# Fused attention, gated MLP and channel mix on one core: accumulator banks for turned blocks, a new layout of the first batch's work, and raw w_k loads behind gate weights

## The chip, the cores and the metric

The kernel runs on one core of a Trainium2 chip. The metric is the device time of one execution in microseconds, the median of several runs. Matmuls run on TensorE (PE in the profile, its weight loads PEld), the rest on VectorE (DVE), ScalarE (ACT) and GpSimd (POOL). SyncE (SP) issues every DMA of this kernel, in order.

## The reference

Three parts, all in fp32, with B = 4 batches, H = 8 heads, S = 576 positions, D = 64, model width 512, inner width 1024:

```python
# attention with a decay bias
cum = cumsum(max(s, 0)); bias = min(-(cum[q] - cum[k]), 0)
attn = softmax(where(causal, -1e9, q @ k.T / 8 + bias)); x = attn @ v      # -> [B, S, 512]
# gated MLP
h = gelu_tanh(x @ w_in); u, v = h[:, :512], h[:, 512:]
v_s = w_sg @ layernorm(v, g_ln) + b_sg          # mixes positions
x = x + (u * v_s) @ w_out
# channel mix
xk, xr = lerp(x, shift(x), mu_k), lerp(x, shift(x), mu_r)
out = sigmoid(xr @ w_r) * (max(xk @ w_k, 0) ** 2 @ w_v)
```

## The kernel before

**Precision.** A product of two fp32 operands is made of fp32r parts: a rounded high part and the rest (`split_lo`, L69: x minus high, 1 instruction). `gemm3` (L374) adds high·high, high·low and low·high in one PSUM bank. Weights come in as 64-bit words; `convert` (L75) makes them into high and low parts with three ScalarE instructions (L77, L82, L88) and three VectorE ones (L83, L85, L70).

**Attention** (`attn_pair`, L213). 16 pairs of heads, four per batch; the first batch has pairs 0 to 3. For each head the transposed k and q come in (`kq`), upper and lower halves are copied and shifted by DMA into `qa`, `ka`, `QB`, `KB`, low parts are split off (mostly on GpSimd), and the sums of `s` go into spare rows by two small DMAs. Scores of a block row of 128 queries go to a PSUM bank `sc`; VectorE adds the mask and takes the minimum (L284), ScalarE takes the exponential with its sum (L292). Each block row is then turned by TensorE against the identity (L307, L310, L318) into a bank `tp` (or `tq`) and copied to `pt1` or `pt2` (L312 to L321). `i` counts the block rows 0 to 4; the last is 64 rows of both heads together. The sums are turned too (`rt`, L324), inverted, written to DRAM and read back broadcast (`rb`), and multiply `x_t` at L361.

**Gated MLP** (`moe1`, L381), once for each batch: `xs` is the split x (L395, L396), `xq` its last 64 columns side by side (L398). Five `v` products, gelu, statistics (L424, L425), a power on GpSimd (L426, L427), the normalisation at L428, cast (L430) and split (L432). Then eight `u` products, eight spatial products `sg`, the gate (L468 to L471) and eight `o` products. The weights of u and o come in eight blocks `wc` of 512 KB through three buffers: the first batch converts them itself (`first_wc`, L179) and writes them to DRAM, the later ones load them from there (`load_wc`, L513). Blocks 0 to 3 serve u, 4 to 7 serve o. For the first three batches gelu is made of Square, Tanh and two VectorE steps (L501); the last batch uses the chip's own gelu.

**Banks.** PSUM has eight banks: three `sc`, two `tp`, three `acc`. `bank` (L367) gives `moe1` only `acc` in the first three batches and all eight in the last one. `tq`, `pv` and, in the first batch, fourth and fifth block tiles and `rt` are `acc` as well; in later batches those tiles and `rt` are `tp`.

**Order.** `attention_until` (L544) interleaves the generators: attention leads the MLP by `LEAD` heads (0.75), with costs `A_COST` and `E_COST`. The prologue (L151) runs beside the first batch's attention: step 0 to 3 convert the four parts of `w_in` for v, 4 to 6 the first three `wc`, 7 to 11 load and split the spatial weights (`spatial`, L198). `PRO` (L542) says at how many finished heads the first seven steps come; step 2 also writes the sums to DRAM and loads four constants (L160). A scheduler then places the instructions of all engines by a timeline of its own; `after` (L495) adds an order to it, no semaphore.

**Channel mix.** `late(i)` (L577) loads the raw w_k (i below 8) and w_r through two buffers `lraw` and converts them; conversions 4 to 7 are held behind the last normalised cast of the last batch. `mixed` makes x tiles, `dense` the products k and r; the rest is a product in seven parts with w_v.

```python
    PRO = [0, 0] + [0.5 + 0.75 * i for i in range(5)]
    ...
            attention_until((b + 1) * H + LEAD + RATE[b] * H * e_done / E_COST)
            if pro is not None and next(pro, None) is None:
                pro = None
    ...
        raw = lk.tile([P, 512, 2], U32, tag="lraw", name=f"lraw{i}", bufs=2)
        nc.sync.dma_start(out=raw.rearrange("p n c -> p (n c)"), in_=src.bitcast(U32))
```

Of the kernel before, what the change touches and what calls it, by code (L numbers as in the profile page):

```python
# [8 lines left out]
F32 = mybir.dt.float32  # L9
F32R = mybir.dt.float32r  # L10
U32 = mybir.dt.uint32
AF = mybir.ActivationFunctionType
ALU = mybir.AluOpType

B, H, S, D = 4, 8, 576, 64
DM, DFF = 512, 1024
FH = DFF // 2
P = 128
# [12 lines left out]
QS = 256  # L31
# [7 lines left out]
def fused_kernel(ctx, tc, kqT, vL, s, w_in, g_ln, w_sgT, b_sg, w_out, mu_k, mu_r, w_k, w_v, w_r, out):  # L39
    nc = tc.nc  # L40
# [5 lines left out]
    wscr = dram.tile([8, P, 2 * KD * P], F32R, tag="wscr", name="wscr")  # L46
# [18 lines left out]
    def f32(ap):  # L65
        return ap.bitcast(F32)


    def split_lo(eng, lo, x, hi):  # L69
        eng.tensor_tensor(out=lo, in0=x, in1=f32(hi), op=ALU.subtract)  # L70
# [25 lines left out]
    psum1 = banks1.enter_context(tc.tile_pool(name="psum1", bufs=3, space=bass.MemoryType.PSUM))  # L96
# [17 lines left out]
    wsg = [ew.tile([P, NT, S], F32R, tag=f"wsg{i}", name=f"wsg{i}") for i in range(2)]  # L114
# [83 lines left out]
    def spatial(k):  # L198
        raw = ep.tile([P, TW1], F32, tag="tmp", name=f"wsr{k}", bufs=3)[:, :S]
        if k < 4:  # L200
            nc.sync.dma_start(out=raw, in_=w_sgT[k * P:(k + 1) * P])
        else:
            nc.sync.dma_start(out=raw[0:64], in_=w_sgT[512:])
            nc.sync.dma_start(out=raw[64:128], in_=w_sgT[512:])
        nc.scalar.copy(wsg[0][:, k], raw)
        split_lo(nc.gpsimd, wsg[1][:, k], raw, wsg[0][:, k])

    xT = {}

# [3 lines left out]
    def attn_pair(b, hp):  # L213
# [3 lines left out]
        for hh in range(2):  # L217
            h = 2 * hp + hh
            hd = b * H + h

            kq = at.tile([P, S], F32, tag="kq", name=f"kq{hd}", bufs=2)
            nc.sync.dma_start(out=kq, in_=kqT[b, h])
            i = hd % (NSET + 1) if first else hd % NSET
            qb, kb = QB[i], KB[i]

            csrc = cr[hd:hd + 1] if b == 0 else cumd[hd]
            nc.sync.dma_start(out=f32(qb[1:4:2]), in_=f32(csrc))
            last_row[0] = nc.sync.dma_start(out=f32(kb[0:3:2]), in_=f32(csrc))
            if i < NSET:
                qa = at.tile([P, S], F32R, tag="qa", name=f"qa{hd}")  # L230
                ka = at.tile([P, S], F32R, tag="ka", name=f"ka{hd}")
            else:
                qa, ka = qaf, kaf
            (nc.scalar.copy if hd < 2 else nc.gpsimd.tensor_copy)(qb[64:128], kq[64:128])  # L234
            (nc.vector.tensor_copy if 1 < hd < 4 else nc.scalar.copy)(ka[0:64], kq[0:64])  # L235
            nc.sync.dma_start(out=f32(qa[0:64]), in_=f32(qb[64:128]))
            nc.sync.dma_start(out=f32(ka[64:128]), in_=f32(ka[0:64]))
            lo = nc.vector if hd in (0, 2) else nc.gpsimd
            split_lo(lo, qa[64:128], kq[64:128], qb[64:128])
            split_lo(lo, kb[64:128], kq[0:64], ka[0:64])  # L240
            ops.append((qa, ka, qb, kb))
            if hh == 0:
                vf = at.tile([P, 2, NT, D], F32, tag="vf", name=f"vf{pr}", bufs=2)
                nc.sync.dma_start(out=vf, in_=vL[b][:, h:h + 2])
                x_t = ep.tile([P, S], F32, tag="xT", name=f"xT{pr}", bufs=8)
                xT[(b, hp)] = x_t
            yield 0
# [14 lines left out]
        for hh, i in steps:  # L262
# [38 lines left out]
            if i == 0:  # L301
                st0 = st
                continue
            tag = "acc" if first and i > 2 else "tp"
            tp = psum1.tile([P, 512], F32, tag=tag, name=f"tp{pr}_{hh}_{i}", bufs=3 if tag == "acc" else 2)
            if i == 1:
                nc.tensor.transpose(tp[:, 0:P], st0[:, 0:P], ident)  # L307
# [3 lines left out]
            if i == 1:  # L311
                (nc.vector.tensor_copy if first and not hh else nc.scalar.copy)(pt1[:, hh], tp[:, :QS + P])  # L312
            elif i < 4:
                (nc.vector.tensor_copy if i == 2 and not first else nc.scalar.copy)(
                    pt2[:, hh, :i + 1, q0 - QS:w - QS], tp[:, :(i + 1) * P].rearrange("p (j m) -> p j m", m=P))
            else:
                tp4 = psum1.tile([P, 512], F32, tag="acc", name=f"tq{pr}", bufs=3)
                nc.tensor.transpose(tp4[:, 0:P], st[:, 512:640], ident)  # L318
                for a in range(2):
                    nc.scalar.copy(pt2[:, a, :4, q0 - QS:], tp.rearrange("p (j a m) -> p a j m", j=4, a=2)[:, a])  # L320
                nc.vector.tensor_copy(pt2[:, :, 3, 0:64], tp4[:, :P].rearrange("p (a m) -> p a m", a=2))  # L321
            yield (i + 1) * 200
        rt = psum1.tile([P, 512], F32, tag="acc" if first else "tp", name=f"rt{pr}", bufs=3 if first else 2)
        nc.tensor.transpose(rt[:9, :P], sm, ident)  # L324
        rc = at.tile([9, P], F32, tag="rc", name=f"rc{pr}")
        nc.vector.tensor_scalar_add(rc, rt[:9, :P], SUM_EPS)
# [54 lines left out]
    def moe1(b):  # L381
# [13 lines left out]
            nc.scalar.copy(xs[0][:, k], xT[(b, k)])  # L395
            split_lo(nc.vector if b == 0 else nc.gpsimd, xs[1][:, k], xT[(b, k)], xs[0][:, k])  # L396
        for i in range(2):
            nc.vector.tensor_copy(xq[:, :, i], f32(xs[i][:, :, 512:]))  # L398
        yield 0
        v = ep.tile([P, NT, FH], F32, tag="v", name=f"v{b}")  # L400
        st6 = ep.tile([P, NT, 6], F32, tag="st6", name=f"st6_{b}")
# [3 lines left out]
        for t in range(NT):  # L405
# [13 lines left out]
            else:  # L419
# [5 lines left out]
            nc.vector.bn_aggr(out=mv[:m, t], in_=st6[:m, t])  # L425
            nc.gpsimd.tensor_scalar_add(rstd[:m, t:t + 1], mv[:m, t, 1:2], LN_EPS * GS * GS)  # L426
            nc.gpsimd.tensor_tensor(out=rstd[:m, t:t + 1], in0=rstd[:m, t:t + 1], in1=mhalf[:m, 0:1], op=ALU.pow)  # L427
            nc.vector.tensor_scalar(out=v[:m, t], in0=v[:m, t], scalar1=mv[:m, t, 0:1], scalar2=rstd[:m, t:t + 1],  # L428
                                    op0=ALU.subtract, op1=ALU.mult)
            last_cast[0] = nc.scalar.copy(vn[0][:m, t], v[:m, t])  # L430
            if t < 4:
# [59 lines left out]
    exps = []  # L491
    last_gate = [None]
    last_cast = [None]

    def after(late, early):  # L495
        tc.add_manual_dep(late.ins, early.ins.name, mybir.DependencyInfo(mybir.DependencyClass.NoSync, mybir.DependencyReason.DATA),
                          reason="order")
# [15 lines left out]
    def load_wc(b, c):  # L513
        if b == 0:
            if c >= 3:
                first_wc(c)
            return wc0[c]
        wc = ew.tile([P, 2, KD * P], F32R, tag="wc", name=f"wc{b}_{c}", bufs=3)
        nc.sync.dma_start(out=f32(wc.rearrange("p a f -> p (a f)")), in_=f32(wscr[c]))
        return wc  # L520


# [10 lines left out]
    LATE = (2, 4)  # L533
    A_COST = 2 * 3136 + 6600 + 8000 + 128
    E_COST = V_W * 56 * 512 + U_W * 8 * 12 * 288 + O_W * 8 * 12 * 288 + S_W * 8 * 14 * 288
    LEAD = 0.75

    pro = prologue()
    a_it = a_stream()
    a_done = 0.0  # L540

    PRO = [0, 0] + [0.5 + 0.75 * i for i in range(5)]  # L542

    def attention_until(n):  # L544
        nonlocal a_done
# [31 lines left out]
    def late(i):  # L577
        hi, lo = ([t[:, i % KD, i // KD * 512:(i // KD + 1) * 512] for t in wk] if i < 8 else [t[:, i - 8] for t in wr])
        src = w_k[i % KD * P:(i % KD + 1) * P, i // KD * 512:(i // KD + 1) * 512] if i < 8 else w_r[(i - 8) * P:(i - 7) * P]
        raw = lk.tile([P, 512, 2], U32, tag="lraw", name=f"lraw{i}", bufs=2)  # L580
        nc.sync.dma_start(out=raw.rearrange("p n c -> p (n c)"), in_=src.bitcast(U32))
        y = lk.tile([P, CH], F32, tag="ltmp", name=f"ly{i}", bufs=4)
        t = lk.tile([P, CH], F32, tag="ltmp", name=f"lz{i}", bufs=4)
        convert(hi, lo, raw, y, t.bitcast(U32), nc.vector, low=mhalf[:, 0:1], hold=last_cast[0] if 4 <= i < 8 else None)
# [298 lines left out]
```

## Time and profile before

| | |
|---|---|
| median of the timed runs | 663.49 us (3 runs, 661.94 to 665.26) |
| profiled execution | 665.93 us, its span 664.1 us |
| TensorE busy | 626.1 us, 94% |
| VectorE, ScalarE, GpSimd busy | 471.3, 416.6, 216.9 us |
| mean granted clock of TensorE | 0.982 |

The span runs from the first to the last instruction. A row of the profile gives start, length, engine, line, operation, output tile <- input tiles, shape and count; in brackets the idle time of the engine before it and what ended that. Window rows give the busy time of each engine in a stretch. The granted clock is a share of 2.4 GHz, so 0.50 is 1.2 GHz.

### The profile page before, as it was taken

How to read it: one execution, taken by the hardware profiler on the slowest of the kernel's cores; microseconds unless marked ns; L12 is line 12 of the kernel's file. 1: busy time of each engine (PE TensorE's matmuls, PEld its weight loads, DVE VectorE, ACT ScalarE, POOL GpSimd, SP SyncE). 2: the span in 40 equal slices, each digit the busy share in tenths (PEclk: the TensorE clock that was granted, in tenths of full speed). 3: DMA queues.
4: the chain of work that ended last, by engine and by line, in shares of the span. 5: the costliest groups of instructions: out<-in, count | busy, mean ns of one | idle time of the engine just before them, and what ended most of it. 6: DMA issues, size and time to landing. Idle time of an engine off the chain costs nothing.

```text
span 664.1 us, 11486 instructions
## 1 busy us (share of the span) xinstructions
PE 626.1 (94%) x3912; PEld 553.0 (83%) x3912; DVE 471.3 (71%) x1002; ACT 416.6 (63%) x938; POOL 216.9 (33%) x217
## 2 busy tenths in 40 slices
PE   2869999889999999999999979999999999999997
PEld 1647778679988999877998879988888988999997
DVE  7868679967559835478732678778875969577864
ACT  5879879766638846358732574577755788553530
POOL 7364667467526578348461220000000000000000
PEclk9789999989999999999999989999999999999999
DMA  7675554554462531924403853677654693546643
GB/s 219 187 251 156 163 172 133 154 182 126 153 209 69 175 107 53 292 53 131 140 12 79 295 191 128 198 226 226 246 167 152 207 375 135 169 182 188 229 142 119
DMA packets 56458, 112.74 MB, mean 170 GB/s; under 512 B 7680, under 2 KB 20624, under 8 KB 56400
## 3 DMA queue, kind: packets, MB, share of 16 engines
q1 hardware_dynamic: 56400, 112.01, 53.0%
q8 instruction: 31, 0.51, 0.3%
q14 instruction: 27, 0.22, 0.1%
HBM read 74.46 MB, written 28.02 MB: 154 GB/s over the span
## 4 chain that ended last, share of the span: by engine, by line
PE 77%; DMA 8%; DVE 6%; ACT 3%; issue 2%; SPq 1%; POOL 1%; DVEq 0%; POOLq 0%; ACTq 0%
PE k L377 15%; PE sg L377 9%; PE psa L781 8%; PE r L377 7%; PE o L377 6%; PE pv L346 5%; PE u L377 5%; PE tp L310 4%; PE v L377 4%; PE psb L781 4%; PE sc L257 4%; PE sc L258 3%; PE psc L781 2%; DMA ka<-ka 1%; DMA rb<-rdram 1%
## 5 line engine op out<-in xcount | busy, mean ns | idle before, releaser
L377 PE MATMUL k<-x,wk 128*128 128x512 f32 (+1 forms) x480 | 98.9, 368 | 0.0
L377 PEld LDWEIGHTS k<-x,wk 128*128 128x128 f32 x480 | 83.6, 189 | 14.9
L292 ACT ACTIVATE st<-st,mx 128x384 f32<-128x384 f32 (+4 forms) x128 | 74.8, 586 | 16.1 <-DVE mx L284 15.7
L284 DVE CUSTOM_DVE_ANT_0 st<-sc,mask 128x512 f32<-128x512 f32 (+3 forms) x128 | 62.7, 504 | 21.4 <-PE sc L258 13.8
L257 PE MATMUL sc<-ka,qa 128*128 128x512 f32 (+3 forms) x180 | 62.0, 358 | 16.4 <-DMA ka<-ka 13.6
L377 PE MATMUL sg<-wsg,vn 128*128 128x288 f32 x448 | 62.6, 296 | 2.4 <-DVE u L511 2.4
L377 PEld LDWEIGHTS sg<-wsg,vn 128*128 128x128 f32 x448 | 60.2, 188 | 3.3 <-DVE u L511 2.6
L258 PE MATMUL sc<-KB,QB 128*128 128x512 f32 (+3 forms) x180 | 57.5, 340 | 0.0
L257 PEld LDWEIGHTS sc<-ka,qa 128*128 128x128 f32 x180 | 33.9, 190 | 22.4 <-ACT ka L235 12.0
L310 PE MATMUL tp<-ident,st 128*128 128x128 f32 x316 | 51.6, 283 | 0.9 <-ACT st L292 0.9
L346 PE MATMUL pv<-pt,vf 128*64 128x320 f32 (+4 forms) x448 | 50.6, 364 | 0.0
L377 PE MATMUL r<-x,wr 128*128 128x512 f32 (+1 forms) x240 | 49.5, 368 | 0.0
L377 PEld LDWEIGHTS r<-x,wr 128*128 128x128 f32 x240 | 41.9, 189 | 7.5
L70 POOL TENSOR_TENSOR qa<-kq,QB 64x576 fp32r<-64x576 f32 x29 | 45.4, 1567 | 5.4 <-ACT QB L234 3.4
L377 PE MATMUL v<-wv,xs 128*128 128x512 f32 x192 | 47.1, 396 | 0.0
L377 PE MATMUL u<-xs,wc 128*128 128x288 f32 x288 | 42.9, 304 | 4.2 <-DMA wc<-wscr 4.2
L346 PEld LDWEIGHTS pv<-pt,vf 128*64 128x64 f32 x448 | 29.2, 136 | 19.5 <-issue 2.7
L70 POOL TENSOR_TENSOR KB<-kq,ka 64x576 fp32r<-64x576 f32 x29 | 42.8, 1474 | 6.5 <-ACT ka L235 4.4
L377 PEld LDWEIGHTS u<-xs,wc 128*128 128x128 f32 x288 | 40.7, 195 | 4.8 <-DMA wc<-wscr 4.4
L310 PEld LDWEIGHTS tp<-ident,st 128*128 128x128 f32 x316 | 39.6, 146 | 5.3 <-ACT st L292 1.7
L377 PE MATMUL o<-gh,wc 128*128 128x288 f32 x192 | 41.3, 299 | 0.6 <-DVE y L486 0.6
L377 PEld LDWEIGHTS v<-wv,xs 128*128 128x128 f32 x192 | 35.3, 188 | 7.5 <-issue 0.3
(190 smaller groups left out, 1422.7 us busy)
## 6 DMA issues: line engine op xcount, KB each, us to landing
wc<-wscr SPq DMA_DIRECT2D x24, 512.0 KB
kq<-in_kqT_dram SPq DMA_DIRECT2D x32, 288.0 KB
kr<-kdram SPq DMA_DIRECT2D x12, 768.0 KB
kdram<-k SPq DMA_DIRECT2D x16, 512.0 KB
yt<-ydram SPq DMA_DIRECT2D x24, 257.0 KB
vf<-in_vL_dram SPq DMA_DIRECT2D x16, 320.0 KB
ydram<-y SPq DMA_DIRECT2D x16, 288.5 KB
gt<-gdram SPq DMA_DIRECT2D x12, 384.0 KB
```

Source lines behind the costliest of these rows:

```text
L70: eng.tensor_tensor(out=lo, in0=x, in1=f32(hi), op=ALU.subtract)
L257: nc.tensor.matmul(sc[:m, :c1 - c0], qa[:, q], ka[:, c0:c1], start=True, stop=False)
L258: nc.tensor.matmul(sc[:m, :c1 - c0], qb[:, q], kb[:, c0:c1], start=False, stop=True)
L284: mi = nc.vector.tensor_tensor_reduce(out=st[:, c0:c1], in0=sc[:, :n], in1=mk, op0=ALU.add, op1=ALU.min, scale=-SCALE, scalar=mx[:, 0:1] i ...
L292: e = nc.scalar.activation(st[:, :w], st[:, :w], AF.Exp, bias=mx[:, last:last + 1], scale=-1.0, accum_out=sm[:, i + 5 * (hh == 1):i + 5 * ...
L310: nc.tensor.transpose(tp[:, c:c + P], st[:, j * P:(j + 1) * P], ident)
L346: both.append(nc.tensor.matmul(acc[64 * a:64 * a + 64, o:n], vf[:, a, kk], pt, start=(kk == 0), stop=(kk == nk - 1)))
L377: nc.tensor.matmul(acc, a, w_, start=(i == 0), stop=(i == n - 1))
L781: nc.tensor.matmul(to[:, :HW], l, r, start=(start and i == 0), stop=(i == len(mms) - 1), skip_group_check=True)
```

## The change

- The tiles of the fourth and fifth block rows are `acc` for pairs 0 to 4 (before: 0 to 3), and `rt` is `acc` for all pairs.
- Third-block copies of pairs 4 to 15 go from VectorE to ScalarE, fourth-block copies of pairs 6 to 15 from ScalarE to VectorE. The two copies of the fifth block become one.
- The first batch: the split of the spatial weights goes from GpSimd to VectorE, the normalisation from VectorE to GpSimd, the copy of the second head's `QB` from ScalarE to GpSimd. The `xq` copies of all batches go from VectorE to ScalarE.
- Prologue steps 2 to 6 come at 1, 2, 3, 4 and 5 heads instead of 0.5, 1.25, 2, 2.75 and 3.5. `LEAD` is 0.9 instead of 0.75.
- Raw w_k loads 2 and 3 are ordered behind the load of the last batch's third `wc` block, 4 to 7 behind that of its fourth.

```diff
@@ spatial
         nc.scalar.copy(wsg[0][:, k], raw)
-        split_lo(nc.gpsimd, wsg[1][:, k], raw, wsg[0][:, k])
+        split_lo(nc.vector, wsg[1][:, k], raw, wsg[0][:, k])
@@ attn_pair
-            (nc.scalar.copy if hd < 2 else nc.gpsimd.tensor_copy)(qb[64:128], kq[64:128])
+            (nc.scalar.copy if hd < 1 else nc.gpsimd.tensor_copy)(qb[64:128], kq[64:128])
...
-            tag = "acc" if first and i > 2 else "tp"
+            tag = "acc" if pr < 5 and i > 2 else "tp"
...
-                (nc.vector.tensor_copy if i == 2 and not first else nc.scalar.copy)(
+                (nc.vector.tensor_copy if i == 3 and pr > 5 else nc.scalar.copy)(
                     pt2[:, hh, :i + 1, q0 - QS:w - QS], tp[:, :(i + 1) * P].rearrange("p (j m) -> p j m", m=P))
...
-                for a in range(2):
-                    nc.scalar.copy(pt2[:, a, :4, q0 - QS:], tp.rearrange("p (j a m) -> p a j m", j=4, a=2)[:, a])
+                nc.scalar.copy(pt2[:, :, :4, q0 - QS:], tp.rearrange("p (j a m) -> p a j m", j=4, a=2))
...
-        rt = psum1.tile([P, 512], F32, tag="acc" if first else "tp", name=f"rt{pr}", bufs=3 if first else 2)
+        rt = psum1.tile([P, 512], F32, tag="acc", name=f"rt{pr}", bufs=3)
@@ moe1
-            nc.vector.tensor_copy(xq[:, :, i], f32(xs[i][:, :, 512:]))
+            nc.scalar.copy(xq[:, :, i], f32(xs[i][:, :, 512:]))
...
-            nc.vector.tensor_scalar(out=v[:m, t], ...)
+            nc.gpsimd.tensor_scalar(out=v[:m, t], ...) if b == 0 else nc.vector.tensor_scalar(out=v[:m, t], ...)
@@
+    last_wc = []
@@ load_wc
-        nc.sync.dma_start(out=f32(wc.rearrange("p a f -> p (a f)")), in_=f32(wscr[c]))
+        i = nc.sync.dma_start(out=f32(wc.rearrange("p a f -> p (a f)")), in_=f32(wscr[c]))
+        if b == B - 1:
+            last_wc.append(i)
@@
-    LEAD = 0.75
+    LEAD = 0.9
...
-    PRO = [0, 0] + [0.5 + 0.75 * i for i in range(5)]
+    PRO = [0, 0] + [1 + 1 * i for i in range(5)]
@@ late
-        nc.sync.dma_start(out=raw.rearrange("p n c -> p (n c)"), in_=src.bitcast(U32))
+        d = nc.sync.dma_start(out=raw.rearrange("p n c -> p (n c)"), in_=src.bitcast(U32))
+        if 2 <= i < 8:
+            after(d, last_wc[2 if i < 4 else 3])
```

## Rows read from the trace of the kernel before

**Rows 1.** the page, busy time, share of the span and instructions of each engine

```profile
PE 626.1 (94%) x3912; PEld 553.0 (83%) x3912; DVE 471.3 (71%) x1002; ACT 416.6 (63%) x938; POOL 216.9 (33%) x217
```

**Rows 2.** windows: stretch, length, busy PE PEld DVE ACT POOL (count), clock, DMA, GB/s

```profile
0.00:150.00 150.00, 120.86 (x776) 97.26 (x776) 118.20 (x309) 118.79 (x310) 89.96 (x87) 0.93 0.60 181
...
25.50:31.20 5.70, 5.70 (x24) 5.13 (x24) 4.42 (x12) 5.24 (x16) 4.54 (x4) 0.52 0.47 128
100.00:130.10 30.10, 27.13 (x192) 22.95 (x192) 29.55 (x78) 27.76 (x78) 20.89 (x20) 1.00 0.50 153
130.10:136.00 5.90, 5.88 (x23) 5.30 (x24) 3.80 (x12) 3.19 (x9) 3.13 (x3) 0.50 0.26 100
...
150.00:350.00 200.00, 199.47 (x1433) 177.06 (x1432) 127.54 (x348) 122.36 (x315) 116.88 (x113) 1.00 0.42 125
...
392.90:397.60 4.70, 4.70 (x24) 4.70 (x25) 3.77 (x6) 3.99 (x8) 0.00 (x0) 0.65 0.46 159
...
393.90:423.40 29.50, 29.50 (x212) 29.24 (x211) 24.54 (x43) 15.49 (x26) 0.30 (x3) 0.96 0.44 143
```

**Rows 3.** TensorE's waits over the span: total us, times, longest

```profile
PE sc L257 <- POOL KB L70: 4.8, 1, 4.8
PE u L377 <- DMA wc<-wscr: 4.2, 1, 4.2
PE sc L257 <- DMA ka_f<-ka_f: 2.9, 1, 2.9
PE sg L377 <- DVE u L511: 2.4, 1, 2.4
PE sc L257 <- DMA qa<-QB: 1.3, 1, 1.3
PE u L377 <- DVE u L511: 1.1, 1, 1.1
...
PE tq L318 <- DVE u L511: 0.5, 1, 0.5
```

**Rows 4.** timeline of SyncE's DMA issues, 340 to 410 us: start, length

```profile
372.37 13.90 SPq L581 DMA_DIRECT2D lraw<-in_w_k_dram  x4
386.37 2.57 SPq L519 DMA_DIRECT2D wc<-wscr  x3
```

**Rows 5.** timeline of TensorE, 345 to 430 us: start, length

```profile
378.89 9.70 PE L377 MATMUL u<-xs,wc 128*128 128x288 f32 x72
...
392.90 4.90 PE L377 MATMUL u<-xs,wc 128*128 128x288 f32 x24 [4.19 <-DMA wc<-wscr]
...
426.69 3.57 PE L377 MATMUL k<-x,wk 128*128 128x512 f32 x15
```

**Rows 6.** timeline of VectorE, 364 to 430 us

```profile
393.22 0.69 DVE L70 TENSOR_TENSOR vn<-v,vn 64x512 fp32r<-64x512 f32 x1 [0.68 <-ACT vn L430]
...
422.76 0.68 DVE L70 TENSOR_TENSOR x<-yx,x 128x512 fp32r<-128x512 f32 x1
```

**Rows 7.** timeline of SyncE's DMA issues, 0 to 50 us

```profile
17.93 0.80 SPq L164 DMA_DIRECT2D sraw<-in_w_in_dram  x2
...
20.81 0.59 SPq L237 DMA_DIRECT2D ka_f<-ka_f  x1
```

**Rows 8.** line 428 on VectorE: 99 to 127 us, then its min/median/max ns

```profile
99.00:127.00 28.00, 4.39 (x5) 1.00 0.49 150
...
L428 DVE TENSOR_SCALAR v<-v,mv,rstd x5: 434/531/1660, 100.0 to 124.4; 128x512 f32<-128x512 f32 x4, 64x512 f32<-64x512 f32 x1
```

**Rows 9.** groups of VectorE by shape: busy us, mean ns, idle before

```profile
L314 DVE COPY pt<-tp 128x384 f32<-128x384 f32 x24 | 13.1, 548 | 8.2 <-PE tp L310 8.1
...
L70 DVE TENSOR_TENSOR xs<-xT,xs 128x576 fp32r<-128x576 f32 x4 | 3.4, 844 | 0.7 <-ACT xs L395 0.7
```

**Rows 10.** groups of GpSimd by shape

```profile
L70 POOL TENSOR_TENSOR vn<-v,vn 128x512 fp32r<-128x512 f32 x12 | 16.4, 1367 | 10.1 <-ACT vn L430 9.6
...
L70 POOL TENSOR_TENSOR wsg<-wsr,wsg 128x576 fp32r<-128x576 f32 x5 | 7.2, 1439 | 6.2 <-ACT wsg L205 6.2
```

More of the change, by code (lines that the diff above doesn't have):

```diff
@@ L427, in moe1 @@
             nc.gpsimd.tensor_tensor(out=rstd[:m, t:t + 1], in0=rstd[:m, t:t + 1], in1=mhalf[:m, 0:1], op=ALU.pow)
-            nc.vector.tensor_scalar(out=v[:m, t], in0=v[:m, t], scalar1=mv[:m, t, 0:1], scalar2=rstd[:m, t:t + 1],
+            nc.gpsimd.tensor_scalar(out=v[:m, t], in0=v[:m, t], scalar1=mv[:m, t, 0:1], scalar2=rstd[:m, t:t + 1],
+                                    op0=ALU.subtract, op1=ALU.mult) if b == 0 else nc.vector.tensor_scalar(out=v[:m, t], in0=v[:m, t], scalar1=mv[:m, t, 0:1], scalar2=rstd[:m, t:t + 1],
                                     op0=ALU.subtract, op1=ALU.mult)
```

## The prediction, made before the change was run

> **What bounds the kernel now.** I read the page's busy times first, then the windows, then TensorE's waits, then the timelines around each wait. TensorE is busy for 94% of the span [rows 1], and from 150 to 350 us for 199.47 of 200 us [rows 2]. So a faster VectorE, ScalarE or GpSimd buys time only where TensorE stands still: in the first 150 us, of which it is busy for 120.86, and once more near 390 us. The waits say where [rows 3]: 2.9 us for the shifted keys of the third head, 4.8 us for a GpSimd split, then 1.1, 0.5, 1.3 and 2.4 us between 120 and 145 us (the 0.5 us is the turned block of a pair waiting for the same gelu step as the 1.1 and the 2.4), and 4.2 us for gate weights. The time before the first matmul is left out, for the first two prologue steps stay where they are.
>
> Each longer wait has a second price. The granted clock was 0.52 in the 5.7 us behind the first of them, 0.50 in 130.1 to 136.0 and 0.65 in 392.9 to 397.6, TensorE being busy throughout [rows 2]: half speed and something above it, against 1.00 in the long middle. A stretch of length t at clock c lost about t(1-c): 2.7, 2.9 and 1.6 us. So what can be had at the places that the change touches is 2.9+2.7 early, 5.3+2.9 around 130 us and 4.2+1.6 at the gate weights.
>
> The profiled execution took 665.93 us (span 664.1), the median of the three timed runs is 663.49. I work out differences in the former and take them off the latter.
>
> **A. Raw w_k behind gate weights.** SyncE issues DMAs in order. At 372.37 us it comes to four raw w_k loads and needs 13.90 us for them, since there are two raw buffers and each load waits for an earlier one to be converted; three loads of wc stand behind them and go out only at 386.37 [rows 4]. The first of the three is the fourth weight block of the last batch. TensorE ends the other three blocks at 378.89+9.70 = 388.59 and gets the fourth at 392.90 [rows 5]. In the change, raw loads 4 to 7 come behind that fourth load. Its own condition is that the first weight block is read, a third of the 9.70 us after 378.89, so about 382.1; with 512 KB that took 6.5 us beside other traffic (386.37 to 392.90) it lands by 388.6, on time. Raw loads 2 and 3 come behind the third load, which is issued before 372 anyway: nothing. Conversions 4 to 7 lose nothing either, for they are held until the last normalised cast, ahead of the split at 393.22 [rows 6].
> The wait of 4.2 goes, and with it the slow clock: 24 matmuls in 4.90 us against 9.70/3 = 3.23, so 1.67 us [rows 5]. Together 5.9. Late next: the spatial product needs that split, done at 393.91; TensorE would be at it by 388.59+3.23 = 391.8, and 12 of its 14 matmuls (about 1.6 us) don't need it, so it waits 0.5. That leaves 5.4. Behind it VectorE's chain (conversions, gates, first mixed tile) ends at 422.76+0.68 = 423.4 [rows 6], 3.25 us ahead of the point where k runs undisturbed, 426.69 [rows 5]. If it can't come forward, the gain stops at 3.25; it was busy for 24.54 of the 29.5 us [rows 2], so 5.0 us of idle time are there to be closed, and 2.2 are needed. I take -4.8, ends -3.3 and -5.4.
>
> **B. Prologue steps later.** Steps 2 to 6, counted from 0, go from 0.5, 1.25, 2, 2.75, 3.5 heads to 1, 2, 3, 4, 5. Each moves a 512 KB load, on SyncE also the four constants and the write of the sums, and per step three VectorE and three ScalarE instructions. Before, two such loads stand at 17.93 us, ahead of the third head's shifts, which go out last at 20.81 and land for 25.47 [rows 7]. Without them the head can start right behind the second one. The move also takes VectorE and ScalarE work out of these microseconds, while the copy of the second head's upper q half goes from ScalarE to GpSimd; these I cost at nothing, since the same wait covers them. Ends: 2.9+2.7 = 5.6 gained; or the moved loads land on the next heads and stretch a wait like that of 4.8 by its own length. I take half the gain, -2.8, for the steps have to go somewhere before 60 us.
>
> **C. First batch laid out anew.** VectorE is busy for 29.55 of the 30.1 us from 100 to 130 [rows 2], with the waits of 1.1, 0.5 and 1.3 in them or at their end, and 2.4 behind. The change takes five normalisations off it there, in all 4.39 us [rows 8]. It takes off the two small remainder copies too, and the third-block copies of pairs 4 and 5, four of 0.55 [rows 9]. It puts on five splits of the spatial weights, which come earlier, beside the first v products, where rows 3 show no wait of TensorE for VectorE: by the nearest row, the 128x576 split, 0.84 each [rows 9], hidden there. GpSimd sheds five of 1.44 and gets five normalisations, for which the bounds are VectorE's 0.43 [rows 8] and 1.37, GpSimd's own two-input split of the same width [rows 10]; I take 1.0, so GpSimd is no worse off. Ends: all of 5.3+2.9 = 8.2 gained; or a new wait as long as the longest here, +2.4, if a split falls in VectorE's queue ahead of a gelu step. I take half, -4.0.
> The rows of the normalisation show one thing against it: the same instruction, over 512 columns each time, took from 0.434 to 1.660 us [rows 8], GpSimd being busy for 20.89 of the 30.1 us [rows 2]. I read that as VectorE being held by what GpSimd does beside it. The Trainium skill has such a rule ("SBUF — State Buffer", section "Who interferes with whom"): the two engines share a port pair as an exclusive lock, and a VectorE instruction in its two-port mode, or with two inputs in SBUF, and a GpSimd instruction that reads SBUF hold each other up. By that rule, with which the spread agrees, five more readers on GpSimd where VectorE is fullest could cost it what they spare it, and the sum would be 4.0 us worse; by the totals of the rows alone it stays.
>
> **D. Banks, copies, lead.** The fourth and fifth blocks of pair 4 (three tiles) and the turned sums of pairs 4 to 15 go from the two tp banks to the three acc banks, which the first three batches' products also use. Twelve sums, each until VectorE has read it. At best nothing is lost, and tp is freer; at worst each makes TensorE wait as the gelu did, 1.1 [rows 3]. I take +1.0 in all, near the lower end, as from 150 us on TensorE has hardly waited [rows 2]. From pair 6 on, fourth-block copies (512 columns) go to VectorE and third-block ones (384) to ScalarE, two ScalarE copies become one, attention leads by 0.9 and not 0.75 heads: nothing, covered by TensorE's 199.47 of 200 us; without that cover it would be at most one copy of 0.55 per head [rows 9].
>
> **Sum.** -4.8 -2.8 -4.0 +1.0 = -10.6: the profiled execution goes to 655.3, the median to 652.9. Forecast **653.0**, by itself 647 to 659 (A at -3.3, B and C at -1 each, D at +1, against A at -5.4, B at -4.5, C at -6.5, D at 0).
>
> **Rivals.**
> 1. *The port takes back what VectorE sheds.* C is 0: 656.9. For it: 0.434 against 1.660 for one instruction [rows 8]. Against it: five readers of 1.44 us leave GpSimd shortly before [rows 10]. The rule of the Trainium skill under C speaks for this case.
> 2. *The first batch gives all.* B and C whole, and the wait of 4.8 gone as well: -4.8-5.6-8.2-4.8 = -23.4, so 640. For it: these waits hang together, a late head delays the next. Against it: the moved loads still have to pass.
> 3. *Slower: acc banks.* Three banks hold gelu inputs, block tiles and sums; a sum that waits for VectorE stops the next product, and TensorE takes its matmuls in order. Fifteen tiles at 1.1 us [rows 3] are 16.5; with A, B and C (-11.6) it comes to 668.4. It decides once a sum lies unread for longer than TensorE needs to fill the two other banks. For it: the three gelu waits already seen are of this kind. Against it: each sum is one short read.
> 4. *The prologue only moves the wait.* B's gain is cancelled by a wait of 4.8 added to it, C gives nothing: 663.49-4.8-2.8+4.8+1.0 = 661.7. For it: the last three steps now come near the head of that wait. Against it: they came near it before as well.
> 5. *The w_k order does nothing*, since the scheduler places the raw loads ahead of it elsewhere or their conversions then end late: 657.7.
>
> **Numbers.** Forecast 0.46, rivals 0.15, 0.10, 0.12, 0.12, 0.05. About 0.5%, 3.3 us, can be told from no change here. Faster than 660.2: forecast, 1, 2 and 5, 0.76. Within: rival 4, 0.12. Slower than 666.8: rival 3, 0.12. The range 643 to 663 takes in B and C near their upper ends and rival 4, and leaves out rival 3 and the far end of rival 2, about 0.2.
>
> **What would show it.** A: wc of the last batch issued by 383 us (on the old scale) and ahead of the fifth raw w_k load, no wait of u for wc, clock 1.00 behind it, the first undisturbed k some 5 us earlier measured from the start of the last batch's products. B: no raw load between the second and the third head's shifts, no wait for ka_f, clock near 1.00 from 25 to 31 us. C: VectorE below 29 of 30 us around 100 to 130, the waits for gelu steps shorter. D: no new waits of TensorE for sums' readers after 150 us. The forecast is wrong if TensorE's idle time in the first 150 us stays at 29 us (150 less 120.86), if the wait at the gate weights moves to the gates rather than goes, or if acc waits appear in the middle batches.

## The result and the profile after

The changed kernel took 655.48 us (median of 4 runs, 654.81 to 657.20) against 664.24 for the kernel before, run beside it (4 runs): 8.8 us less, ratio 0.9854, 95% interval 0.9818 to 0.9890. The forecast was 653.0 within 643 to 663, so time and sign are right. The reasons are mostly not, as will be seen: A and B are worth nothing in the full change that these runs can tell, and C and D, which together make the whole gain, don't do so apart (B alone was not run).

The profiled execution after took 657.2 us (span 655.4). Its busy times, from the page (same columns as [rows 1]):

```profile
PE 620.6 (95%) x3912; PEld 547.0 (83%) x3912; DVE 478.0 (73%) x990; ACT 415.2 (63%) x933; POOL 217.5 (33%) x218
```

TensorE is busy for 5.5 us less with the same 3912 matmuls, so in this execution much of the gain is in how fast they ran. The windows, with the columns of [rows 2], say where:

```profile
0.00:150.00 150.00, 121.11 (x805) 96.73 (x806) 127.42 (x310) 122.39 (x313) 95.56 (x90) 0.98 0.60 181
100.00:130.10 30.10, 27.63 (x197) 23.56 (x196) 26.87 (x71) 28.83 (x79) 24.06 (x21) 1.00 0.45 133
130.10:136.00 5.90, 5.07 (x39) 3.99 (x38) 5.90 (x17) 5.90 (x16) 4.83 (x3) 1.00 0.70 232
150.00:350.00 200.00, 198.60 (x1427) 175.49 (x1426) 127.71 (x341) 119.42 (x308) 114.01 (x113) 1.00 0.42 124
350.00:430.00 80.00, 79.29 (x520) 73.56 (x521) 55.94 (x103) 45.09 (x83) 7.96 (x16) 1.00 0.61 200
```

The last stretch is one that was not shown of the kernel before; there the same view has

```profile
350.00:430.00 80.00, 75.23 (x505) 70.14 (x504) 51.72 (x97) 38.66 (x70) 10.05 (x18) 0.98 0.55 179
```

In the first 150 us TensorE still stands still for 28.9 us (150 less 121.11; 29.1 before), but the clock rose from 0.93 to 0.98 and the half-clock stretch of 130.1 to 136.0 is gone. VectorE, which the change was to relieve, is busier there, 127.42 against 118.20 us. From 350 to 430 us TensorE has 4.1 us more of work done (79.29 against 75.23). TensorE's largest waits over the span, without the one for the first matmul:

```profile
PE sc L257 <- DVE mx L284: 8.2, 8, 2.9
PE sc L257 <- DMA ka_f<-ka_f: 2.0, 1, 2.0
PE sg L376 <- DVE vn L70: 1.5, 1, 1.5
PE v L376 <- DVE v L512: 1.4, 1, 1.4
PE tp L307 <- ACT st L292: 1.4, 1, 1.4
PE u L376 <- DVE u L512: 1.4, 2, 1.1
PE sc L257 <- DVE pt L320: 1.2, 1, 1.2
PE o L376 <- DMA wc<-wscr: 0.7, 1, 0.7
```

Against [rows 3]: the 4.8 us for GpSimd's split and the 4.2 for gate weights are gone, the waits for gelu steps are smaller, and 8.2 us for row maxima (mx) have come, most of them in the first 100 us. SyncE's issues at the two places of [rows 4, 7]:

```profile
18.57 0.80 SPq L164 DMA_DIRECT2D sraw<-in_w_in_dram  x2
21.39 0.60 SPq L237 DMA_DIRECT2D ka_f<-ka_f  x1
...
378.27 0.32 SPq L520 DMA_DIRECT2D wc<-wscr  x1
378.69 0.85 SPq L584 DMA_DIRECT2D lraw<-in_w_k_dram  x2
381.45 3.51 SPq L520 DMA_DIRECT2D wc<-wscr  x2
```

The two raw loads are still ahead of the third head's shifts, though the prologue asks for them later. The last batch's fourth gate weights now go out ahead of the fifth raw w_k load, and TensorE runs its gate and spatial products (compare [rows 5]) without a gap:

```profile
375.03 12.75 PE L376 MATMUL u<-xs,wc 128*128 128x288 f32 x95
387.62 15.02 PE L376 MATMUL sg<-wsg,vn 128*128 128x288 f32 x112
```

GpSimd's normalisations, from the groups by shape between 85 and 155 us (busy us, mean ns, idle before), which answer to [rows 8]:

```profile
L427 POOL TENSOR_SCALAR v<-v,mv,rstd 128x512 f32<-128x512 f32 x4 | 9.1, 2272 | 0.2
```

They take 2.27 us each, where the forecast had 1.0.

### The profile page after: what moved, and what is told of

Its sections match the earlier page's. It is cut to its first block, busy times and chain, and to the rows that moved or that the text cites. A ratio compares the mean times of both kernels' runs of the same rounds, so it can differ in the third digit from the quotient of the medians.

```text
span 655.4 us, 11462 instructions
## 1 busy us (share of the span) xinstructions
PE 620.6 (95%) x3912; PEld 547.0 (83%) x3912; DVE 478.0 (73%) x990; ACT 415.2 (63%) x933; POOL 217.5 (33%) x218
## 4 chain that ended last, share of the span: by engine, by line
PE 81%; DVE 7%; DMA 7%; issue 2%; SPq 1%; ACT 1%; DVEq 0%; ACTq 0%
PE k L376 15%; PE sg L376 9%; PE psa L786 8%; PE r L376 8%; PE o L376 7%; PE v L376 7%; PE pv L345 6%; PE u L376 5%; PE tp L310 4%; PE psb L786 4%; PE sc L257 4%; PE sc L258 3%; PE psc L786 2%; DMA rdram<-rc 2%; DMA wsr<-in_w_sgT_dram 1%
## 5 line engine op out<-in xcount | busy, mean ns | idle before, releaser
L70 POOL TENSOR_TENSOR qa<-kq,QB 64x576 fp32r<-64x576 f32 x29 | 44.0, 1517 | 2.1
L376 PE MATMUL u<-xs,wc 128*128 128x288 f32 x288 | 41.3, 298 | 1.1 <-DVE u L512 1.1
L605 ACT ACTIVATE yx<-yt,mu 128x64 f32<-128x64 f32 (+4 forms) x64 | 30.5, 530 | 17.7 <-DMA yt<-ydram 17.7
```

What stands on the lines that cost most here:

```text
L376: nc.tensor.matmul(acc, a, w_, start=(i == 0), stop=(i == n - 1))
L605: i = nc.scalar.mul(t[:, s0:s1], yt[:, s0 + d:s1 + d], mu[:, r, 1, k:k + 1])
```

## The experiments

Twelve kernels, each timed in five rounds against the kernel before. The table gives medians and ratios, and three things worked out from the windows 0:40, 40:100, 100:150, 150:350 and 350:430 of each kernel's one profiled execution: TensorE's idle time (length less busy) up to 150 us, from 150 to 350, and from 350 to 430, and the time lost to the clock, busy x (1 - clock), summed over the five. That last column is rough and on the low side, as a stretch's clock is a mean that takes in TensorE's idle time: by the mean granted clock of the whole span (0.982 and 0.994) the kernel before lost 12.0 us and the full change 3.9.

| kernel | median us | ratio to before (95%) | idle to 150 | 150-350 | 350-430 | clock |
|---|---|---|---|---|---|---|
| before | 664.24 | 1 | 29.1 | 0.5 | 4.8 | 9.9 |
| full change | 655.48 | 0.9854 (0.9818-0.9890) | 28.9 | 1.4 | 0.7 | 2.5 |
| A alone | 661.24 | 0.9950 (0.9925-0.9975) | 29.8 | 0.5 | 2.0 | 7.2 |
| all but A | 655.57 | 0.9868 (0.9830-0.9905) | 27.2 | 1.2 | 0.8 | 2.5 |
| old prologue steps | 657.15 | 0.9890 (0.9857-0.9922) | 28.9 | 1.8 | 0.9 | 4.1 |
| normalisation on VectorE | 662.74 | 0.9972 (0.9947-0.9997) | 27.4 | 3.4 | 0.8 | 4.1 |
| C alone | 664.89 | 1.0012 (0.9983-1.0042) | 28.1 | 6.3 | 0.2 | 7.4 |
| D alone | 658.13 | 0.9917 (0.9882-0.9952) | 29.7 | 2.5 | 0.8 | 8.5 |
| normalisation alone | 673.13 | 1.0160 (1.0118-1.0201) | 25.9 | 6.8 | 3.1 | 10.5 |
| all but A, old q copy | 655.38 | 0.9885 (0.9850-0.9921) | 25.5 | 1.3 | 0.7 | 3.7 |
| C and D | 656.53 | 0.9847 (0.9809-0.9885) | 25.7 | 1.2 | 0.5 | 7.3 |
| all but A, old banks | 661.70 | 0.9931 (0.9904-0.9958) | 28.8 | 5.0 | 1.3 | 3.6 |
| all but A, old lead | 656.07 | 0.9843 (0.9804-0.9882) | 27.1 | 1.1 | 0.5 | 0.9 |
| D and normalisation | 657.83 | 0.9875 (0.9834-0.9915) | 29.4 | 0.1 | 1.0 | 5.0 |

The runs were made in three groups, beside which the kernel before had medians of 663.87, 664.75 and 665.83 us; so compare ratios. Profiles are single executions: that of the full change (657.20 us) is the longest of its four, that of D alone (663.54) the longest of its eight (from 657.32), that of run 10 (664.42) near the upper end of its twelve (659.06 to 665.11).

How far a cell of the table can be trusted shows in kernels whose traces have TensorE's matmuls in the same order (by the names of the tiles). The kernel before and run 1 agree up to 388 us: 29.1 and 29.8 us of idle time to 150 us, 0.5 and 0.5 from 150 to 350. The full change, run 2 and run 3 agree up to 403 us: 28.9, 27.2 and 28.9, then 1.4, 1.2 and 1.8. So differences of 4 to 6 us between 150 and 350 us stand clear, and differences of 2 us before 150 don't. The clock varies more. The four executions of the full change had mean granted clocks of 0.994 (the profiled one, 657.20 us), 0.987, 0.992 and 0.986 (the fastest, 654.81 us). Over all executions the clock averaged 0.984 to 0.986 for the kernel before, by group, 0.990 for the full change, 0.987 for D alone, 0.992 for run 4 and 0.994 for run 10, and the last two are among the slower kernels.

**1. Part A alone.** The kernel before with the two hunks that name `last_wc`:

```diff
+        i = nc.sync.dma_start(out=f32(wc...), in_=f32(wscr[c]))
+        if b == B - 1:
+            last_wc.append(i)
...
+        if 2 <= i < 8:
+            after(d, last_wc[2 if i < 4 else 3])
```

> The kernel before with one part of the change alone: raw w_k loads 2 and 3 behind the third load of gate weights of the last batch, 4 to 7 behind the fourth. Theory (A pays by itself, as in the two traces, where the lead of the changed kernel grew by 6.0 us between 371 and 400 us and 1.1 came back by 450): 664.2 - 4.9 = 659.3, between 658.5 and 660.0, with no wait of the gate products (u) for wc and the granted clock at 1.00 behind it. Rival (the growth came from the last batch being reached in another state, since the work before it was laid out anew): 662 to 664.

Measured 661.24, ratio 0.9950: 2.6 us faster by the medians, 3.3 by the ratio (its interval: 1.7 to 5.0). The median lies between the theory's range and the rival's, at about half of the theory's 4.9. TensorE's timeline of the last batch shows both halves of it:

```profile
378.89 12.88 PE L377 MATMUL u<-xs,wc 128*128 128x288 f32 x96
...
408.16 0.53 PE L377 MATMUL o<-gh,wc 128*128 128x288 f32 x2 [0.62 <-ACT gh L469]
...
420.41 0.40 PE L377 MATMUL o<-gh,wc 128*128 128x288 f32 x1 [0.84 <-DMA wc<-wscr]
423.69 4.48 PE L377 MATMUL k<-x,wk 128*128 128x512 f32 x19
```

The gate products start at the very time of [rows 5], 378.89, and run through to 391.77, which before they reached at 392.90+4.90 = 397.80: 6.0 us. But undisturbed k comes at 423.69 and not 426.69: 3.0 us are given back, to ScalarE's gate cast and the output weights among others.

**2. Everything but A.** The changed kernel without those last two lines.

> The changed kernel without the order of the raw w_k loads, so B, C and D alone. Theory (the parts add up): 655.5 + 4.9 = 660.4, the raw loads ahead of the fourth gate weights again, and a u waiting about 4 us for wc near 390 us. Rival (in the new layout the loads stand elsewhere by themselves): 655 to 657.

Measured 655.57 against 655.48 with A: the rival. SyncE's issues in this kernel:

```profile
368.90 5.42 SPq L584 DMA_DIRECT2D lraw<-in_w_k_dram  x2
375.40 6.68 SPq L520 DMA_DIRECT2D wc<-wscr  x3
```

Two raw loads stand ahead of the fourth gate weights, not four as in [rows 4], and no gate product waits. Nothing in B, C or D names these loads. The program's order is written by a scheduler when it is built, and the other parts make it place them otherwise: C alone and D alone (runs 5 and 6) lose this wait too. So A removes a wait which the rest of the change has removed already.

**3. Old prologue steps** in the changed kernel.

```diff
-    PRO = [0, 0] + [1 + 1 * i for i in range(5)]
+    PRO = [0, 0] + [0.5 + 0.75 * i for i in range(5)]
```

> The changed kernel with the prologue's steps at 0.5 to 3.5 heads, as before. Theory (B moved nothing that counts: in the changed kernel's trace the two raw loads still went out ahead of the third head's shifts, at 18.57 against 21.39 us): 655.5, within 1 us, and the wait for ka_f and the half clock near 30 us as they are. Rival (the forecast's term B, hidden by a loss elsewhere in the first 50 us): 2.8 slower, 658.3.

Measured 657.15, ratio 0.9890: 1.7 us above the full change by the medians, 2.4 by the ratios, between the theory (within 1 us of 655.5) and the rival (658.3), and the two intervals overlap over about half their length. So this run alone decides nothing. Runs 8 and 9 below differ in B's steps alone as well, and there the old steps are the faster ones (0.9885 with the new, 0.9847 with the old): no gain of B's can be told from nothing. In run 3 TensorE's 3912 matmuls come in the very order of the full change, the profile's idle time up to 150 us is the same 28.9, and the two raw loads go out at 18.44 us, where the full change has 18.57:

```profile
18.44 0.80 SPq L164 DMA_DIRECT2D sraw<-in_w_in_dram  x2
```

**4. Normalisations on VectorE again** in the changed kernel.

```diff
-            nc.gpsimd.tensor_scalar(out=v[:m, t], ...) if b == 0 else nc.vector.tensor_scalar(out=v[:m, t], ...)
+            nc.vector.tensor_scalar(out=v[:m, t], ...)
```

> The changed kernel with the first batch's five normalisations on VectorE again. Theory (they take 2.27 us each on GpSimd and slow VectorE's instructions beside them, so VectorE gains nothing by shedding 0.43 us of its own): 653.5 to 655.5, VectorE's other instructions in 100 to 150 us shorter than now. Rival (term C as forecast, the relief of VectorE is what pays): 2 to 4 slower, 657.5 to 659.5, with a clock of 0.5 near 130 us as before.

Measured 662.74, ratio 0.9972 against 0.9854 for the full change: 1.2% slower. The theory fell, and the rival named the wrong place: up to 150 us idle time and lost clock together are the same as in the full change (31.5 and 31.4). It loses later, in the middle batches, which the edit doesn't touch:

```profile
150.00:350.00 200.00, 196.57 (x1395) 171.63 (x1394) 125.96 (x336) 116.73 (x300) 114.25 (x111) 1.00 0.42 123
```

TensorE gets through 1395 matmuls there against 1427. Its idle time is 3.4 us against 1.4; the rest is longer busy time, 4.2 us over the span (624.8 against 620.6), for which no cause is shown.

**5. Part C alone,** the kernel before with these lines:

```diff
-        split_lo(nc.gpsimd, wsg[1][:, k], raw, wsg[0][:, k])
+        split_lo(nc.vector, wsg[1][:, k], raw, wsg[0][:, k])
...
-                (nc.vector.tensor_copy if i == 2 and not first else nc.scalar.copy)(
+                (nc.vector.tensor_copy if i == 3 and pr > 5 else nc.scalar.copy)(
...
-            nc.vector.tensor_copy(xq[:, :, i], ...)
+            nc.scalar.copy(xq[:, :, i], ...)
...
+            nc.gpsimd.tensor_scalar(out=v[:m, t], ...) if b == 0 else ...
```

> The kernel before with part C alone (normalisations of the first batch on GpSimd, spatial splits on VectorE, remainder copies on ScalarE, third-block copies of all pairs to ScalarE and fourth-block copies from pair 6 on to VectorE). The program's own order now has two raw w_k loads ahead of the last batch's fourth gate weights, where the kernel before has four. Theory (any such re-laying shifts the loads, so the wait of 4.2 us and its half clock go without part A, and the first batch gives the 3.9 us seen between 137 and 160 us): 664 - 3.9 - 4.5 = 655.5, between 654 and 657. Rival (the wait goes, but C's gain in the first batch is port-bound and belongs to the other parts): 659 to 660. Second rival (the wait stays): 660 or more.

Measured 664.89, ratio 1.0012: no gain at all. The time is that of the second rival, but not for its reason: the wait for gate weights did go (idle from 350 to 430 us is 0.2). TensorE stands still between 150 and 350 us instead. The window, and TensorE's waits in it:

```profile
150.00:350.00 200.00, 193.67 (x1366) 168.63 (x1366) 126.75 (x335) 116.02 (x309) 114.30 (x107) 0.99 0.43 127
```

```profile
PE u L377 <- DVE u L512: 2.2, 2, 1.5
PE sc L257 <- DVE mx L284: 1.7, 3, 1.0
PE sc L257 <- DMA qa<-QB: 1.7, 1, 1.7
```

These are waits for gelu steps, row maxima and shifted queries of the middle batches; before, that stretch had 0.5 us of idle time [rows 2].

**6. Part D alone,** the kernel before with the new banks, one copy and lead:

```diff
-            tag = "acc" if first and i > 2 else "tp"
+            tag = "acc" if pr < 5 and i > 2 else "tp"
...
-        rt = psum1.tile([P, 512], F32, tag="acc" if first else "tp", ...)
+        rt = psum1.tile([P, 512], F32, tag="acc", ...)
...
-    LEAD = 0.75
+    LEAD = 0.9
```

> The kernel before with part D alone (turned sums of all pairs and fourth and fifth blocks of pair 4 in the accumulator banks, one copy in place of two, lead 0.9). Its order has two raw w_k loads in front of the last batch's fourth gate weights too. Theory (D costs nothing by itself and its shift of the order removes the wait for gate weights, nothing in the first batch): 664 - 4.5 = 659.5, between 658 and 661. Rival (the forecast's D, a cost of 1.0 with the wait unchanged): 665. Rival (acc banks stop the next products): 668.

Measured 658.13, ratio 0.9917: the theory. The part that was forecast as a cost measures more by itself than A or C, though its interval overlaps that of A.

**7. The normalisations on GpSimd alone,** the kernel before with the last line of 5.

> The kernel before with the five normalisations of the first batch on GpSimd and nothing else. Theory (they are what part C lives by, as taking them back cost 7 us in the changed kernel): 656 to 657, TensorE's waits for gelu steps between 100 and 150 us below 2 us in all (5.3 before) and no half clock at 130 us. Rival (what counted there was the order of the middle batches, and the normalisations themselves give VectorE nothing, 2.27 us each on GpSimd): only the wait for gate weights goes, 659 to 661.

Measured 673.13, ratio 1.0160: slower, which neither foresaw. Again it is the middle batches:

```profile
150.00:350.00 200.00, 193.20 (x1359) 168.14 (x1358) 124.62 (x333) 119.17 (x306) 115.79 (x110) 0.99 0.43 125
```

and the half clock of the first batch is still there (clock loss 10.5 us in all), though the waits for gelu steps from 100 to 150 us did fall below the theory's 2 us, to 0.4. TensorE is busy for 631.1 us of the span, 5.0 more than before. Of its waits from 150 to 350 us, three are at the banks `tp` themselves: a turned block that waits until VectorE has read the sums of a pair (L326), and a block and a sum that wait for the copy of an earlier block (L314), 2.1 of the 6.8 us (the longest, 2.8, the profile puts down to no engine):

```profile
PE tp L307 <- DVE rc L326: 1.1, 1, 1.1
PE tp L310 <- DVE pt L314: 0.7, 1, 0.7
PE rt L324 <- DVE pt L314: 0.3, 1, 0.3
```

**8. All but A, with the second head's upper q half copied by ScalarE** as before (`hd < 2` for `hd < 1`). Its order is that of run 2 save for some ten lines, so this edit hardly touches what the scheduler does.

> The changed kernel without part A and with the second head's upper q half copied by ScalarE, as before. The program's order is that of the run without A but for some ten lines in the first 30 us. Theory (GpSimd's work on the second head at 10 to 15 us is what made VectorE's steps there take 1.2 to 1.8 us and TensorE wait 1.9 for a maximum at 15.5): 1 to 1.5 faster than the run without A, 654.3. Rival (the time is set by the shifted keys of the third head, which land when SyncE's queue lets them): same, 655.6.

Measured 655.38: the same, the rival. The waits for row maxima fell from 4.1 to 3.3 us in all, and those for the third and sixth head's shifted keys rose from 3.6 to 5.1.

```profile
PE sc L257 <- DMA ka_f<-ka_f: 5.1, 2, 2.9
PE sc L257 <- DVE mx L284: 3.3, 5, 1.1
```

**9. C and D together,** the lines of 5 and 6 in the kernel before, no A and no B.

> The kernel before with parts C and D, without A and B. Theory (C and D pay together: D's accumulator banks and lead keep the middle batches free of the waits that C alone brought there, 6.3 us of idle from 150 to 350 us, and B and A give nothing on top): 655.5 to 657, idle time from 150 to 350 us below 2 us, clock 1.00 from 100 to 150 us. Rival (B's later steps are needed too): 659 or more, above D alone.

Measured 656.53, ratio 0.9847: the theory, and the whole of the gain. The middle batches are nearly free of waits again (1.2 us idle):

```profile
150.00:350.00 200.00, 198.77 (x1428) 175.92 (x1427) 127.58 (x339) 120.01 (x308) 113.15 (x113) 1.00 0.42 124
```

One point missed: the clock from 100 to 150 us was 0.97, not 1.00.

**10. All but A, with the old banks** (the first two changes of 6 taken back).

> The changed kernel without part A and with the old banks: turned sums of pairs 4 to 15 and the late blocks of pair 4 in the two tp banks again. Theory (the banks are the part of D that C needs): the middle batches wait again, some 5 us of idle from 150 to 350 us, 660 to 662. Rival (it is the lead): 655 to 657.

Measured 661.70, ratio 0.9931: the theory. Idle time of 5.0 us in the middle batches, with these as the largest waits from 150 to 350 us:

```profile
150.00:350.00 200.00, 195.03 (x1387) 170.45 (x1388) 128.92 (x342) 121.34 (x312) 115.86 (x112) 1.00 0.42 127
```

```profile
PE tp L310 <- ACT st L292: 2.1, 4, 0.9
PE o L376 <- DVE y L486: 1.0, 1, 1.0
PE tq L318 <- DVE ga L464: 0.6, 1, 0.6
```

None of them is a wait for a `tp` bank to be read: the blocks wait for their own exponentials (`st`), the product and `tq` for readers of `acc`. So here the old banks don't cost their time the direct way that run 7 shows. TensorE's order, too, is another than in run 2 from 76 us on.

**11. All but A, with the old lead** (0.75).

> The changed kernel without part A and with attention leading by 0.75 heads as before. Theory (the banks matter, the lead hardly): 655 to 657, idle from 150 to 350 us below 2.5 us. Rival (the lead of 0.9 is what lets the middle batches run without waits): 660 to 662 and some 5 us of idle there.

Measured 656.07, ratio 0.9843: the theory; the lead doesn't count. TensorE's order leaves that of run 2 as well, at 103 us, without a loss: another order by itself need not cost anything.

```profile
150.00:350.00 200.00, 198.90 (x1419) 174.86 (x1418) 125.13 (x340) 119.86 (x308) 114.48 (x112) 1.00 0.41 125
```

**12. D and the normalisations,** the lines of 6 and the last of 5 in the kernel before.

> The kernel before with part D and, of part C, the five normalisations on GpSimd alone. Theory (inside C it is the normalisations that pay once D is there, as taking them out of the changed kernel cost 7 us): 655 to 657, no half clock from 100 to 150 us. Rival (they cost by themselves, 8 us more alone, and D makes up only part of that): 661 to 666, with idle in 150 to 350 us.

Measured 657.83, ratio 0.9875: 0.8 above the theory's upper end, far from the rival. The middle batches are as full as they can be:

```profile
150.00:350.00 200.00, 199.87 (x1440) 176.31 (x1439) 125.63 (x345) 122.35 (x306) 120.95 (x115) 1.00 0.41 123
```

What cost 1.6% alone costs nothing that shows beside the new banks. Whether it gains something over D alone (0.9917) can't be told, as the intervals overlap.

No kernel here beats the change by more than the intervals; runs 2, 8, 9 and 11 are level with it and change less.

## Why the prediction was right or wrong

**The sum.** -10.6 forecast, -8.8 measured. It came out near because errors met: A and B, 7.6 together, give nothing in the full change that can be told from nothing, and D, put down as a loss, pays by itself, and its banks are what C needs (run 10 against run 11, beside which it was timed: 0.9931 and 0.9843). The failed step is the one under the sum itself: four terms were priced apart and added. Alone, C and D measured 1.0012 and 0.9917, which would add up to 0.9929; together 0.9847. Alone, A measured 0.9950; on top of the rest, 0.9868 became 0.9854, well inside either interval.

**A (-4.8, ends -3.3 and -5.4).** The mechanism holds where the wait exists: alone it removed the wait of 4.2 us and the slow clock behind it, 6.0 us against the 5.9 worked out. The limit behind it was drawn too kindly: the prediction gave 3.25 as the gain if VectorE's chain can't come forward, and took 4.8. It was 3.0 in the trace, 2.6 by the medians and 3.3 by the ratio, at that end. The waits that run 1 names behind the gate products are ScalarE's cast (0.62 us) and output weights (0.84); that VectorE's chain set the limit isn't shown. In the full change the step failed otherwise: the wait was read as a property of the kernel, and it was one of one order. Rival 5 (the w_k order does nothing, 0.05) came true in its first reason, that the scheduler places the raw loads elsewhere, but not in its time of 657.7: the wait was gone without A, so nothing was missing from the gain.

**B (-2.8).** Failed at "without them the head can start right behind the second one". The loads did not leave: 18.57 us, ahead of the shifts at 21.39, and 18.44 with the old steps (run 3). The wait for ka_f went from 2.9 to 2.0 us, and 8.2 us of waits for row maxima came, against 0.7 before. That fits rival 4's half, a wait that only moves, but one profile can't show it: run 2, with the same TensorE order there, has 3.6 and 4.1 us of these two. From run 2 to run 8 one grew and the other fell, while the median stayed the same.

**C (-4.0).** Neither the size nor the reason is borne out. By the count of matmuls in windows from the start, the changed kernel reached its 700th matmul at 134.6 us and the kernel before at 137.6, which looks like C's size. But C alone reached it at 136.4, 1.2 us ahead, and run 4, with the normalisations back on VectorE, at 132.3. The idle time up to 150 us didn't shrink in the full change. What went is the half clock of 130 to 136 us, in this execution. Two prices failed. A normalisation takes 2.27 us on GpSimd, not 1.0. And VectorE was not relieved: from 100 to 130 us its busy time fell to 26.87, below the 29 that the forecast asked for, but over the first 150 us it rose by 9.2. What the sum left out altogether is what C does to the middle batches: alone, it has 5.8 us more idle time there than the kernel before, and some 1.9 of lost clock (busy 193.67 at 0.99), against 4.6 of idle and 1.5 of clock saved at the gate weights. How much of this is VectorE's or GpSimd's load and how much the order isn't shown, since each edit changed both.

**Rival 1, the port.** It gave 656.9, close to the measured time, and is not borne out as the cause. On VectorE the normalisation is indeed stretched: [rows 8] have 0.434 to 1.660 us for one shape, and its mean between 85 and 155 us was 816 ns in run 4 and 848 in D alone. In the trace of the kernel before the shortest one ran while GpSimd stood still (timelines of VectorE and of GpSimd, 99 to 127 us):

```profile
111.56 0.43 DVE L428 TENSOR_SCALAR v<-v,mv,rstd 128x512 f32<-128x512 f32 x1
...
112.82 1.62 POOL L70 TENSOR_TENSOR vn<-v,vn 128x512 fp32r<-128x512 f32 x1 [2.37 <-ACT vn L430]
```

But moving it to GpSimd didn't tax VectorE's other work in a set way. The second of VectorE's three steps of the weight conversion, from the groups by shape between 85 and 155 us of D alone and then of D with the normalisations on GpSimd:

```profile
L85 DVE SCALAR_TENSOR_TENSOR wy<-wy 128x256 uint32<-128x256 uint32 x8 | 6.6, 824 | 0.1
```

```profile
L85 DVE SCALAR_TENSOR_TENSOR wy<-wy 128x256 uint32<-128x256 uint32 x8 | 3.9, 490 | 0.0
```

It was shorter with more work on GpSimd; between run 4 and the full change it goes the other way (778 and 819). The Trainium skill's rule ("SBUF — State Buffer", section "Who interferes with whom"), that the two engines lock each other out of a shared port pair, agrees with the spread of the normalisation. That moving a reader to GpSimd costs VectorE's other work a set amount, as the rival had it, these runs don't bear out; that it goes by which instructions happen to lie beside each other would fit them, and isn't shown. C beside D measures 0.7% (0.9917 to 0.9847), where this rival had none, but the two intervals just touch.

**D (+1.0) and rival 3 (acc banks, 668).** The sign of the term failed: alone, D is worth 5.5 us by its ratio (0.0083 x 664.75; by the interval 3.2 to 7.8). The prediction put "nothing is lost, and tp is freer" as the best case, since TensorE hardly waited from 150 us on. But that 0.5 us of idle time belonged to the kernel as it stood. Put the runs in four classes by who normalises the first batch and which banks hold the sums, and read the idle time from 150 to 350 us:

| | old banks | new banks |
|---|---|---|
| VectorE normalises | 0.5 (before), 0.5 (run 1) | 2.5 (run 6), 3.4 (run 4) |
| GpSimd normalises | 6.3 (5), 6.8 (7), 5.0 (10) | 1.4 (full), 1.2 (2), 1.8 (3), 1.3 (8), 1.2 (9), 1.1 (11), 0.1 (12) |

With the old banks the move of the normalisations costs the middle batches 4.5 to 6.3 us; with the new ones it takes waits away. The forecast priced the move in the left column's top cell and added the rest. Runs 10 and 11 put it on the banks and not on the lead. Rival 3's mechanism, a product stopped by an unread sum, is not among the full change's waits; with the old banks, run 7 has a turned block stopped by one (1.1 us). Open stays whether the banks act by themselves or by leading the scheduler to another order. For the first speak the 2.1 us of waits at `tp` in run 7, for the second that runs 5 and 10 name none of that kind; no run holds the order fixed while it swaps the banks. Nor is it shown where all of D's own 5.5 us lie, as its one profile, the longest of its executions, has only the 4.0 of idle time and the 1.5 of clock at the gate weights to its credit, and 2.0 more idle time in the middle batches against it.

**What the marks said.** The forecast named idle time of 29 us in the first 150 us as a sign against itself; it stayed at 28.9, and rightly warned that B and C did not work as told. Rival 2 (640), most of whose gain lay there, is out by the same number.

## What to carry to other kernels

Where the order of a program is written by a scheduler, a wait seen in a trace belongs to that order: before pricing a fix, look at what stands ahead of the waiting transfer, and ask whether any other part of the change moves it. Test a change of several parts both ways, each part alone and each part left out, for parts that do nothing or harm alone (the normalisations, +1.6%) can be free beside another (the banks). Before work is moved between engines in one stage, look at the buffers of the stages behind it: with the old banks this kernel lost there what it had gained. And before a clock that changed in one profile is counted as a gain, look at the clock of the other executions.

## What was not expected of the hardware

- A subtract-and-multiply of 128x512 with two per-partition scalars took 2.11 to 2.65 us on GpSimd (means of four in ten kernels), against 0.434 us at best and some 0.8 at the mean on VectorE. It is longer than GpSimd's two-input split of the same width (1.31 us beside it in the full change, 1.37 in [rows 10]).
- TensorE's busy time for the same 3912 matmuls ran from 620.1 to 631.1 us, and the clock explains only part of it: less what the mean granted clock of each span lost, the kernel before has 614.1 us, run 12 has 615.6, the full change 616.7 and run 4 has 619.5. Some 5 us thus hang on the order in which the same matmuls follow each other, or on what runs beside them; which of the two isn't shown, and the ends of matmuls are modelled in the profile.
- The granted clock fell at other places in other orders: in run 12 nothing was lost in the first 40 us and 5.0 between 40 and 100; in run 11 0.9 in the first 40 and nothing behind. But it also differs where the order doesn't: the kernel before lost 2.0 us in the first 40, and run 1, with the same matmuls in the same order, 0.9.
